# A cross network on one core: bias sums moved and put into another bank, third input block moved, and one row matmul in place of two

## The chip, the cores and the metric

The kernel runs on one core of one Trainium2 chip. The core has five engines that matter here: PE (TensorE, matmuls and their weight loads), DVE (VectorE), ACT (ScalarE), POOL (GpSimd) and SP (SyncE, which here only issues transfers). The metric is the device time of the launch in microseconds (us); a lower time is better. Six runs of the kernel before gave a median of 130.84 us (130.69 to 130.98).

## The reference

The reference is a stack of six cross layers. With `x0` of shape 4096 x 416, weights `ws` of shape 6 x 416 x 416 and biases `bs` of shape 6 x 416, all in bfloat16:

```python
x = x0
for l in range(6):
    x = x0 * (x @ ws[l] + bs[l]) + x
```

Both kernels carry the sum differently. After layer l, the result is x0 times (everything that the layers so far contributed, plus the running sum of the biases). So the kernel leaves the contraction sums of all layers in the accumulators (PSUM) and adds only each layer's new product to them. It needs the running sums of the bias rows, one column per layer, as a per-feature scalar: that is `cb_sb`, and making it is what the text calls the bias sums.

## The kernel before

**Tiling.** Features are on partitions, batch rows on columns. The 4096 rows are cut into NS = 4 blocks of 1024, each in two halves of 512. The 416 features are three chunks of 128 plus a tail of 32. The tail of a block lies in four lanes of 32 partitions, one per quarter (256 rows) of the block. In each lane the first 256 columns hold the lane's own quarter and the second 256 hold its neighbour's quarter (lane g holds the quarter of lane g^1).

**A layer on PE** has these stages, in this order (n = 6s + l counts the 24 layers):

- Half A: nine contraction steps, each of four matmuls side by side in column tiles (128 x 32), 512 columns (`step`, recorded at L201).
- The row phase (L343): the tail's 32 features contracted into the chunks. It runs in four row tiles (32 x 128), one lane each. Part 0 covers chunk 0 (even lanes) and chunk 2 (odd lanes), part 1 covers chunk 1 (even lanes) and the tail's own output (odd lanes). An even lane does one matmul of 512 columns per part. An odd lane does two of 256 columns per part, because the neighbour's quarter sits in the second half of its buffer. So a row phase has 12 matmuls. The last one raises `s_ti`, on which DVE's half A of the layer waits.
- Tail outputs (12 matmuls of 256 columns, L201), which raise `s_to`.
- Half B: nine more steps.

DVE then turns each of the six accumulators into the next `x` with one operation of 128 x 512 (L444): add the bias scalar, multiply by x0. ACT (L496), POOL (L188) and ACT again (L478, `swap_lanes`) do the same for the tail and copy it to the neighbour lanes. The next row phase waits for DVE's six (`s_xb`) and for the swap (`s_sw`).

**The start.** Block 0 is loaded row by row and turned on PE, since its turned form is wanted at once. `xin_sb` holds six groups of 128 rows in three transfers (h = 0, 1 and the "third input block", groups 4 and 5); groups 6 and 7 come turned by a transposing transfer. PE runs 14 filler matmuls (L210), then 12 turns of 128 x 128 (L239) in the order `IN_ORDER`, into six banks, of which DVE copies chunks 0 and 2 (`s_inD`) and ACT chunk 1 (`s_inA`). Then, in PE's order:

1. the bias sums: 16 small matmuls of `bsa_sb` with a triangle of ones `u_sb`, into bank 1 (L248 to L254). They raise `s_cbp`; ACT copies bank 1 to `cb_sb` (L465) and raises `s_cb`;
2. contraction step 0 of half A (k = 0), chunk by chunk. Chunk m = 1 accumulates in bank 1, so it waits for `s_cb` (before m = 1);
3. `third_input()`: 24 matmuls into banks 6, 7 and 3, copied by DVE (L424) and ACT (L475);
4. step k = 1; `tail_inputs()` (16 matmuls, raising `s_tp`; copied by ACT at L482 and DVE at L426, `s_te` and `s_te0`); step k = 2;
5. the row phase of layer 0, behind waits for all copies (`s_inD` 6, `s_inA` 3, `s_te`, `s_te0`, `s_cb`) and for the tail's weights (`s_wt`, `s_wtp`).

The order on each engine is written out by hand. PE works through its program in order, and a wait holds all that is behind it; the same holds for ACT, DVE and POOL. The transfers go out on three queues: SP's, ACT's and POOL's. The tail weights of layer 0 come in four pieces by `load_wt`: lanes 1 and 3 from ACT, lanes 0 and 2 from POOL, where they stand ahead of the four `wc_sb` transfers (L173).

The functions that the diff touches, with the line numbers of the profile:

Of the kernel before, what the change touches and what calls it, by code (L numbers as in the profile page):

```python
# [8 lines left out]
ACTF = mybir.ActivationFunctionType  # L9


def bass_standalone__dcn_v2_cross__recsys_kernel(
# [20 lines left out]
    with ExitStack() as es:  # L33
# [58 lines left out]


        IN_BANKS = ((3, 4, 6), (0, 5, 7))
        IN_ORDER = ((0, 0), (0, 1), (1, 0), (1, 1), (0, 2), (1, 2))
        THIRD = (6, 7, 3)
        HALVES = (slice(0, 64), slice(64, 128))

# [12 lines left out]
        @block.sync  # L111
        def _(sp):
            sp.dma_start(xin_sb[:, 0:2, :], x0_v[:, 0:2, :]).then_inc(s_xin[0], 16)
            sp.dma_start(w_sb[:, 0, 0, :], ws[0, 0:128, :]).then_inc(s_w0, 16)
            sp.dma_start(xin_sb[:, 4:6, :], x0_v[:, 4:6, :]).then_inc(s_xin[2], 16)
            sp.dma_start_transpose(x0T_sb[:, :, 768:SB], x0[768:SB, 0:DF]).then_inc(s_x0T[0], 16)
            for l in range(1, L):
                sp.dma_start(w_sb[:, l, :, :], wmain(l)).then_inc(s_w[l], 16)
                if l == 1:
                    for g in range(4):  # L120
                        load_wt(sp, g, 1, L, s_wt[1])
            for s in range(1, NS):
                sp.dma_start_transpose(
                    x0T_sb[:, :, s * SB:(s + 1) * SB], x0[s * SB:(s + 1) * SB, 0:DF]
                ).then_inc(s_x0T[s], 16)
                sp.dma_start_transpose(
                    x4_sb[:, s - 1:s, :], x0[s * SB:(s + 1) * SB, D - 128:D]
                ).then_inc(s_x4[s - 1], 16)
            for s in range(NS - 1):
                n = (s + 1) * L  # L130
                sp.wait_ge(s_xa, NC * n)
                sp.wait_ge(s_xb, NC * n)
                for c in range(NC):
                    sp.dma_start_transpose(
                        o_sb[:, s * JS:(s + 1) * JS, c * 128:(c + 1) * 128], xo_sb[:, s, c, :]
                    ).then_inc(s_oT, 16)
                sp.wait_ge(s_xt, n)
                sp.dma_start_transpose(ot_sb[:, s, :, :], xot_sb[:, s, :]).then_inc(s_ot, 16)
                sp.wait_ge(s_oT, 16 * NC * (s + 1))
                sp.wait_ge(s_otc, s + 1)  # L140
                sp.dma_start(
                    out_v[:, s * JS:(s + 1) * JS, :], o_sb[:, s * JS:(s + 1) * JS, :]
                ).then_inc(s_out, 16)
            j = (NS - 1) * JS
            sp.wait_ge(s_oeA, 2)
            sp.dma_start(out_v[:, j:j + 4, 0:256], o_sb[:, j:j + 4, 0:256]).then_inc(s_out, 16)
            sp.wait_ge(s_oeA, 3)
            sp.wait_ge(s_oet, 1)
            sp.dma_start(out_v[:, j:j + 4, 256:D], o_sb[:, j:j + 4, 256:D]).then_inc(s_out, 16)
            sp.wait_ge(s_oeD, 1)  # L150
            sp.wait_ge(s_oeA, 4)
            sp.dma_start(out_v[:, j + 4:j + 6, :], o_sb[:, j + 4:j + 6, :]).then_inc(s_out, 16)
            sp.wait_ge(s_out, 16 * (NS + 3))

        @block.gpsimd
        def _(pool):
# [8 lines left out]
                out=u_sb[:, :], in_=ones_sb[0:L + 1, 0:L], pattern=[[1, L]],  # L165
                compare_op=ALU.is_ge, fill=0.0, base=1, channel_multiplier=-1,
            ).then_inc(s_set, 1)
            for g in (0, 2):
                load_wt(pool, g, 0, 1, s_wtp)
            pool.wait_ge(s_zero, 1)  # L170
            for i, (a, b) in enumerate(((0, 1), (1, L))):
                for g in (1, 3):
# [26 lines left out]
        def _(pe):  # L199
# [33 lines left out]
            fill(14)  # L233
            pe.wait_ge(s_set, 1)
            for i, (h, c) in enumerate(IN_ORDER):
                if i in (0, 2):
                    pe.wait_ge(s_xin[h], 16)
                for j in range(2 * h, 2 * h + 2):
                    ins = pe.transpose(  # L239
                        out=psT[:, IN_BANKS[h][c], (j % 2) * 128:(j % 2 + 1) * 128],  # L240
                        in_=xin_sb[:, j, c * 128:(c + 1) * 128], identity=ident[:, :],
                    )
                ins.then_inc(s_inT, 1)

            pe.wait_ge(s_bs, 16)
            pe.wait_ge(s_zero, 2)
            pe.wait_ge(s_set, 2)
            for c in range(NC):  # L248
                for q in range(4):
                    f0 = c * 128 + 32 * q  # L250
                    tile_mm(ps[32 * q:32 * q + 32, 1, c * 8:c * 8 + L], bsa_sb[:, f0:f0 + 32], u_sb[:, :], q, True)
            for q in range(4):
                ins = tile_mm(ps[32 * q:32 * q + 32, 1, NC * 8:NC * 8 + L], bsa_sb[:, DF:D], u_sb[:, :], q, True)
            ins.then_inc(s_cbp, 1)  # L254

            def out_chunk(c):
                for j in range(4):
# [7 lines left out]
            for s in range(NS):  # L265
                for l in range(L):
# [34 lines left out]
                    if n == 0:  # L301
                        pe.wait_ge(s_w0, 16)
                        for k in range(NC):
                            if k == 1:
                                pe.wait_ge(s_w[0], 16)
                                third_input()
                            if k == 2:
                                pe.wait_ge(s_xtl0, 16)
                                tail_inputs()
                            before_a(k)  # L310
                            for m in range(NC):
                                if k == 0 and m == 1:
                                    pe.wait_ge(s_cb, 1)
                                step(m, 0, k)
                    else:
                        if s == 0:
                            pe.wait_ge(s_w[l], 16)
                        chunk(0, 0, before_a)
                        chunk(1, 0)
                        chunk(2, 0)  # L320

                    if n == 0:
                        pe.wait_ge(s_inD, 6)
                        pe.wait_ge(s_inA, 3)
                        pe.wait_ge(s_te, 1)
                        pe.wait_ge(s_te0, 1)
                        pe.wait_ge(s_cb, 1)
                    else:
                        pe.wait_ge(s_xb, NC * n)
                        if l == 0:  # L330
                            pe.wait_ge(s_xt, n)
                            pe.wait_ge(s_te, s + 1)
                        else:
                            pe.wait_ge(s_sw, s * (L - 1) + l)
                    if s == 0 and l < 2:
                        if l == 1:
                            pe.wait_ge(s_wc[1], 32)
                        pe.wait_ge(s_wt[l], (32, 64)[l])
                    if n == 0:
                        pe.wait_ge(s_wtp, 32)  # L340

                    def row(g, dst, lhsT, cols, start):
                        return pe.matmul(  # L343
# [4 lines left out]
                    lo, hi = slice(0, G), slice(G, 2 * G)  # L348
                    for part in range(2):
                        if n == 0 and part == 1:  # L350
                            pe.wait_ge(s_wc[0], 32)
                        for h in range(2):
                            g, wm = 2 * h, slice(part * 128, part * 128 + 128)
                            row(g, ps[:, NC * h + part, :], wt_sb[lane(g), l, wm], slice(0, H), h == 1)
                            g += 1
                            if part == 0:
                                row(g, ps[:, NC * h + 2, hi], wt_sb[lane(g), l, 0:128], lo, h == 1)
                            else:
                                row(g, ps[:, 6 + h, lo], wc_sb[lane(g), l, 0:128], lo, True)
                        for h in range(2):  # L360
                            g = 2 * h + 1
                            if part == 0:
                                ins = row(g, ps[:, NC * h + 2, lo], wt_sb[lane(g), l, 0:128], hi, False)
                            else:
                                ins = row(g, ps[:, 6 + h, lo], wc_sb[lane(g), l, 32:160], hi, False)
                    ins.then_inc(s_ti, 1)
                    if n == 0:
# [90 lines left out]
        def _(act):  # L458
# [2 lines left out]
            act.dma_start(xtl_sb[:, :, :], x0_v[:, 6:JS, DF:D]).then_inc(s_xtl0, 16)  # L461
            for g in (1, 3):
                load_wt(act, g, 0, 1, s_wt[0])
            act.wait_ge(s_cbp, 1)
            act.activation(  # L465
                out=cb_sb[:, :, :],
                in_=ps[:, 1, 0:8 * (NC + 1)].rearrange("p (c e) -> p c e", e=8)[:, :, 0:L], func=ACTF.Copy,
            ).then_inc(s_cb, 1)
            for h in range(2):
                act.wait_ge(s_inT, 2 * h + 2)  # L470
                act.activation(
                    out=x0T_sb[:, 1, h * 256:(h + 1) * 256], in_=psT[:, IN_BANKS[h][1], 0:256], func=ACTF.Copy
                ).then_inc(s_inA, 1)
# [6 lines left out]

            act.wait_ge(s_tp, 1)
            act.activation(out=x0t_sb[:, 0, 0:G], in_=ps[:, 5, 0:G], func=ACTF.Copy).then_inc(s_te, 1)  # L482
            act.wait_ge(s_cb, 1)
            for s in range(NS):
                for l in range(L):
# [75 lines left out]
```

## Time and profile before

| What | Value |
|---|---|
| Median of six runs | 130.84 us (130.69 to 130.98) |
| Time of the profiled execution | 130.98 us |
| Its span, first to last instruction | 129.2 us |
| PE busy | 124.5 us (96% of the span) |
| DVE, ACT, POOL busy | 100.5, 71.3, 23.3 us |
| Mean granted clock of PE | 0.996 |
| Last filler matmul ends, row phase of layer 0 begins | 4.00 us, 8.56 us |
| One layer from then on (row phase to row phase) | 4.88 us, layer 0 to 1: 4.95 us |
| Row phases in the chain | 0.55 us each; layer 0: 0.62, layer 1: 0.66 |

The profiled execution's time is 1.78 us above its span (130.98 less 129.2): what lies outside the first and last instruction. Times inside the profile are counted from the span's start. A group of matmuls in four tiles appears as overlapping records; the distance from one group's start to the next is what it costs, not the duration of one record (0.379 us for 512 columns).

### The profile page before, as it was taken

The numbers are of one execution on the slowest core, as the hardware profiler recorded it, in microseconds if no ns is written. First come the engines' busy times: TensorE is split into PE (matmuls) and PEld (weight loads), VectorE is DVE, ScalarE is ACT, GpSimd is POOL, SyncE is SP. The second block draws the span as 40 slices with busy tenths as digits, with TensorE's granted clock in tenths as the row PEclk, the third lists the DMA queues.
The fourth block names the chain that finished last, engine by engine and source line by source line (L and its number), as shares of the span: only waits on it lengthen the run. The fifth ranks groups of instructions, "written<-read, shape, count | busy, mean of one in ns | idle before, by whom it ended". The sixth has DMA issues, their size and how long they took to land.

```text
span 129.2 us, 5416 instructions
## 1 busy us (share of the span) xinstructions
PE 124.5 (96%) x2454; PEld 64.7 (50%) x2454; DVE 100.5 (78%) x154; ACT 71.3 (55%) x164; POOL 23.3 (18%) x42
## 2 busy tenths in 40 slices
PE   7999999999999999999999999999999999999980
PEld 5654454554545545545545545545545545545550
DVE  2349779779779779779779779779779789789790
ACT  0627356376736456476745555475745555555680
POOL 7802102102102022012012022012022032022130
PEclk9999999999999999999999999999999999999998
DMA  3999899996009808000008534000009907000026
GB/s 99 310 283 306 202 119 223 112 235 62 5 5 106 168 0 269 0 0 5 0 5 164 105 109 160 5 0 0 5 0 89 185 0 264 5 0 5 3 82 186
DMA packets 32918, 12.54 MB, mean 97 GB/s; under 512 B 25338, under 2 KB 32896, under 8 KB 32896
## 3 DMA queue, kind: packets, MB, share of 16 engines
q1 hardware_dynamic: 31488, 11.47, 43.5%
q10 hardware_dynamic: 1184, 0.67, 1.7%
q8 instruction: 19, 0.31, 1.0%
q0 software_dynamic: 224, 0.06, 0.2%
q14 instruction: 3, 0.02, 0.1%
HBM read 2.90 MB, written 3.41 MB: 49 GB/s over the span
## 4 chain that ended last, share of the span: by engine, by line
PE 96%; DVE 1%; issue 0%; DVEq 0%
PE ps L201 82%; PE ps L343 10%; PE ps L210 2%; PE ps L239 1%; DVE o_sb L449 1%; PE ps L393 0%; DVEq L33 0%
## 5 line engine op out<-in xcount | busy, mean ns | idle before, releaser
L444 DVE SCALAR_TENSOR_TENSOR xT_sb<-ps,cb_sb,x0T_sb 128x512 bf16<-128x512 f32 x120 | 80.9, 743 | 16.9 <-PE ps L343 16.9
L201 PE MATMUL ps<-xT_sb,w_sb 128*32 128x512 bf16 (+1 forms) x1680 | 89.0, 364 | 0.0
L201 PEld LDWEIGHTS ps<-xT_sb,w_sb 128*32 128x32 bf16 x1680 | 43.1, 97 | 38.6 <-issue 4.2
L478 ACT ACTIVATE xt_sb<-xt_sb 32x256 bf16<-32x256 bf16 x80 | 33.1, 414 | 16.6 <-POOL xt_sb L188 15.9
L496 ACT ACTIVATE t_sb<-ps,cb_sb 64x256 f32<-64x256 f32 x48 | 22.5, 468 | 30.7 <-PE ps L201 30.4
L188 POOL TENSOR_TENSOR xt_sb<-t_sb,x0t_sb 128x256 bf16<-128x256 f32 x20 | 13.4, 671 | 80.4 <-ACT t_sb L496 80.4
L201 PE MATMUL ps<-x0T_sb,w_sb 128*32 128x512 bf16 (+1 forms) x336 | 18.8, 365 | 0.0
L444 DVE SCALAR_TENSOR_TENSOR xo_sb<-ps,cb_sb,x0T_sb 128x512 bf16<-128x512 f32 x23 | 15.6, 743 | 3.4 <-PE ps L343 3.3
L343 PE MATMUL ps<-xt_sb,wt_sb 32*128 32x512 bf16 (+1 forms) x160 | 12.2, 327 | 0.0
L201 PEld LDWEIGHTS ps<-x0T_sb,w_sb 128*32 128x32 bf16 x336 | 8.4, 97 | 7.4 <-issue 0.8
L509 ACT ACTIVATE x0t_sb<-x_sb 32x256 bf16<-32x256 bf16 x24 | 9.9, 413 | 0.4
L343 PE MATMUL ps<-xt_sb,wc_sb 32*128 32x256 bf16 x80 | 7.7, 268 | 0.0
L343 PEld LDWEIGHTS ps<-xt_sb,wt_sb 32*128 32x128 bf16 x160 | 2.5, 92 | 8.6 <-DVE xT_sb L444 8.5
L188 POOL TENSOR_TENSOR xot_sb<-t_sb,x0t_sb 128x256 bf16<-128x256 f32 x4 | 2.7, 672 | 12.6 <-ACT t_sb L496 12.6
L343 PEld LDWEIGHTS ps<-xt_sb,wc_sb 32*128 32x128 bf16 x80 | 4.0, 93 | 0.4
L210 PE MATMUL ps<-const-bfloat16-1.0 128*128 128x256 bf16 x14 | 3.1, 418 | 0.8 <-PEq L546 0.8
L419 DVE COPY x0T_sb<-ps 128x256 bf16<-128x256 bf16 x4 | 1.1, 292 | 2.8 <-PE ps L239 2.5
L465 ACT ACT_TABLE_LOAD x1 | 1.3, 1283 | 3.5 <-issue 3.5
L210 PEld LDWEIGHTS ps<-const-bfloat16-1.0 128*128 128x128 bf16 x14 | 2.0, 145 | 1.6 <-issue 0.8
L343 PE MATMUL ps<-x0t_sb,wt_sb 32*128 32x512 bf16 (+1 forms) x32 | 2.4, 326 | 0.2 <-issue 0.2
L173 POOL DMA_DIRECT2D wc_sb<-in_ws_dram x4 | 2.2, 548 | 0.0
L517 ACT ACTIVATE o_sb<-ps 128x512 bf16<-128x512 f32 x3 | 1.8, 597 | 0.3 <-PE ps L201 0.3
(41 smaller groups left out, 24.0 us busy)
## 6 DMA issues: line engine op xcount, KB each, us to landing
out_dram<-o_sb SPq DMA_DIRECT2D x3, 832.0 KB, 4.1
w_sb<-in_ws_dram SPq DMA_DIRECT2D x5, 312.0 KB, 5.7
xin_sb<-in_x_dram SPq DMA_DIRECT2D x2, 208.0 KB, 3.5
out_dram<-o_sb SPq DMA_DIRECT2D x1, 256.0 KB, 2.3
xin_sb<-in_x_dram ACTq DMA_DIRECT2D x1, 208.0 KB, 3.3
w_sb<-in_ws_dram ACTq DMA_DIRECT2D x1, 208.0 KB, 3.6
out_dram<-o_sb SPq DMA_DIRECT2D x1, 208.0 KB, 2.3
out_dram<-o_sb ACTq DMA_DIRECT2D x1, 208.0 KB, 2.7
```

Of the source, the lines that this page charges most:

```text
L173: pool.dma_start(wc_sb[lane(g), a:b, 32 * g:32 * g + 32], ws[a:b, DF:D, DF:D].rearrange("l p n -> p l n")).then_inc(s_wc[i], 16)
L188: pool.tensor_tensor(out=dst, in0=t32_sb[:, n % 2, :], in1=x0t_sb[:, s, 0:G], op=ALU.mult).then_inc(s_xt, 1)
L201: return pe.matmul(dst, lhsT=lhsT, rhs=rhs, start=start, stop=True, skip_group_check=True, tile_position=(0, 32 * q),)
L210: pe.matmul(ps[:, 7, 0:256], lhsT=const[:, 0:128], rhs=const, start=True, stop=True)
L239: ins = pe.transpose(out=psT[:, IN_BANKS[h][c], (j % 2) * 128:(j % 2 + 1) * 128], in_=xin_sb[:, j, c * 128:(c + 1) * 128], identity=ident[ ...
L343: return pe.matmul(dst, lhsT=lhsT, rhs=srct[lane(g), cols], start=l == 0 and start, stop=True, skip_group_check=True, tile_position=(32 * ...
L444: dve.scalar_tensor_tensor(out=dst, in0=ps[:, NC * half + c, :], scalar=cb_sb[:, c, l:l + 1], in1=x0T_sb[:, c, o:o + H], op0=ALU.add, op1= ...
L465: act.activation(out=cb_sb[:, :, :], in_=ps[:, 1, 0:8 * (NC + 1)].rearrange("p (c e) -> p c e", e=8)[:, :, 0:L], func=ACTF.Copy,).then_inc ...
L478: ins = act.activation(out=buf[lane(g), G:2 * G], in_=buf[lane(g ^ 1), 0:G], func=ACTF.Copy)
L496: ins = act.activation(out=t32_sb[HALVES[h], n % 2, :], in_=tail(h), func=ACTF.Identity, bias=cb_sb[HALVES[h], NC, l:l + 1],)
L509: ins = act.activation(out=x0t_sb[lane(g), s + 1, swap * G:(swap + 1) * G], in_=x4_sb[96:128, s, r * G:(r + 1) * G], func=ACTF.Copy,)
L517: act.activation(out=o_sb[:, j0:j0 + 4, c * 128:c * 128 + 128], in_=ps[:, c, :].rearrange("p (j d) -> p j d", d=128), func=ACTF.Copy,).the ...
```

## The change

- **Bias sums.** They become a function `bias_sums()`, called after `tail_inputs()`, before step k = 2. They write bank 6 in place of bank 1. Bank 6 holds the third input block's chunk 0 at that time, so they wait for DVE's fifth copy (`s_inD` 5). ACT's copy to `cb_sb` moves behind its tail copy. Chunk m = 1 of step k = 0 no longer waits for `s_cb`; that wait now stands before part 1 of the row phase of layer 0, which overwrites bank 6.
- **Third input block.** `third_input()` moves from before step k = 1 to before step k = 2.
- **Order of the turns.** `IN_ORDER` takes chunk 0 of both halves first, then chunk 1, then chunk 2. The waits for the transfers and of ACT follow.
- **Odd lanes' chunk 2.** In part 0 an odd lane does one matmul of 512 columns, which reads its buffer's two halves in swapped order, in place of two of 256. A row phase then has 10 matmuls, in all 24 layers.
- **One transfer.** The tail weights of lane 0 go from POOL's queue to SP's, behind the third input block and ahead of the transposing transfer.

```diff
-        IN_ORDER = ((0, 0), (0, 1), (1, 0), (1, 1), (0, 2), (1, 2))
+        IN_ORDER = ((0, 0), (1, 0), (0, 1), (1, 1), (0, 2), (1, 2))
...
             sp.dma_start(xin_sb[:, 4:6, :], x0_v[:, 4:6, :]).then_inc(s_xin[2], 16)
+            load_wt(sp, 0, 0, 1, s_wt[0])
...
-            for g in (0, 2):
-                load_wt(pool, g, 0, 1, s_wtp)
+            load_wt(pool, 2, 0, 1, s_wtp)
...
-                if i in (0, 2):
+                if i in (0, 1):
                     pe.wait_ge(s_xin[h], 16)
...
-            pe.wait_ge(s_bs, 16)
-            pe.wait_ge(s_zero, 2)
-            pe.wait_ge(s_set, 2)
-            for c in range(NC):
-                for q in range(4):
-                    f0 = c * 128 + 32 * q
-                    tile_mm(ps[32 * q:32 * q + 32, 1, c * 8:c * 8 + L], bsa_sb[:, f0:f0 + 32], u_sb[:, :], q, True)
-            for q in range(4):
-                ins = tile_mm(ps[32 * q:32 * q + 32, 1, NC * 8:NC * 8 + L], bsa_sb[:, DF:D], u_sb[:, :], q, True)
-            ins.then_inc(s_cbp, 1)
+            def bias_sums():
+                pe.wait_ge(s_bs, 16)
+                pe.wait_ge(s_zero, 2)
+                pe.wait_ge(s_set, 2)
+                pe.wait_ge(s_inD, 5)
+                for c in range(NC + 1):
+                    for q in range(4):
+                        f0 = c * 128 + 32 * q if c < NC else DF
+                        ins = tile_mm(ps[lane(q), 6, c * 8:c * 8 + L], bsa_sb[:, f0:f0 + 32], u_sb[:, :], q, True)
+                ins.then_inc(s_cbp, 1)
...
                             if k == 1:
                                 pe.wait_ge(s_w[0], 16)
+                            if k == 2:
                                 third_input()
-                            if k == 2:
                                 pe.wait_ge(s_xtl0, 16)
                                 tail_inputs()
+                                bias_sums()
                             before_a(k)
                             for m in range(NC):
-                                if k == 0 and m == 1:
-                                    pe.wait_ge(s_cb, 1)
                                 step(m, 0, k)
...
                         pe.wait_ge(s_te0, 1)
-                        pe.wait_ge(s_cb, 1)
...
-                        pe.wait_ge(s_wt[l], (32, 64)[l])
+                        pe.wait_ge(s_wt[l], (48, 64)[l])
                     if n == 0:
-                        pe.wait_ge(s_wtp, 32)
+                        pe.wait_ge(s_wtp, 16)
...
                         if n == 0 and part == 1:
+                            pe.wait_ge(s_cb, 1)
                             pe.wait_ge(s_wc[0], 32)
...
                             if part == 0:
-                                row(g, ps[:, NC * h + 2, hi], wt_sb[lane(g), l, 0:128], lo, h == 1)
+                                pe.matmul(
+                                    ps[:, NC * h + 2, :], lhsT=wt_sb[lane(g), l, 0:128],
+                                    rhs=srct[lane(g), :].rearrange("p (b r) -> p b r", b=2)[:, ::-1, :],
+                                    start=l == 0 and h == 1, stop=True, skip_group_check=True, tile_position=(32 * g, 0),
+                                )
                             else:
                                 row(g, ps[:, 6 + h, lo], wc_sb[lane(g), l, 0:128], lo, True)
                         for h in range(2):
                             g = 2 * h + 1
-                            if part == 0:
-                                ins = row(g, ps[:, NC * h + 2, lo], wt_sb[lane(g), l, 0:128], hi, False)
-                            else:
+                            if part == 1:
                                 ins = row(g, ps[:, 6 + h, lo], wc_sb[lane(g), l, 32:160], hi, False)
...
-            act.wait_ge(s_cbp, 1)
-            act.activation(
-                out=cb_sb[:, :, :],
-                in_=ps[:, 1, 0:8 * (NC + 1)].rearrange("p (c e) -> p c e", e=8)[:, :, 0:L], func=ACTF.Copy,
-            ).then_inc(s_cb, 1)
             for h in range(2):
-                act.wait_ge(s_inT, 2 * h + 2)
+                act.wait_ge(s_inT, h + 3)
...
             act.activation(out=x0t_sb[:, 0, 0:G], in_=ps[:, 5, 0:G], func=ACTF.Copy).then_inc(s_te, 1)
+            act.wait_ge(s_cbp, 1)
+            act.activation(
+                out=cb_sb[:, :, :],
+                in_=ps[:, 6, 0:8 * (NC + 1)].rearrange("p (c e) -> p c e", e=8)[:, :, 0:L], func=ACTF.Copy,
+            ).then_inc(s_cb, 1)
```

## The prediction

> **What bounds the kernel now.** I read the chain that ended last first, then the waits, then two row phases and the start in the timeline. The chain (start us, us, what):
>
> ```profile
> 5.41 2.98 PE ps L201 x91
> 8.39 0.17 issue
> 8.56 0.62 PE ps L343 x8
> 9.18 4.33 PE ps L201 x77
> 13.51 0.66 PE ps L343 x8
> 14.17 4.33 PE ps L201 x84
> 18.49 0.55 PE ps L343 x8
> 19.04 4.33 PE ps L201 x84
> ```
>
> From 8.56 us on nothing but PE stands in it: 0.55 + 4.33 = 4.88 us a layer, to 124.57 us. So a row phase that is shorter by d gives 24 d, if DVE keeps up. The waits:
>
> ```profile
> DVE xT_sb L444 <- PE ps L343: 16.9, 20, 1.1
> PEld ps L343 <- DVE xT_sb L444: 8.5, 20, 0.4
> PEld ps L201 <- issue: 5.0, 24, 0.2
> ```
>
> The second line looks as if DVE held PE before each row phase. It doesn't: in the trace's records the first row weight load comes 0.307 us after the last column-tile matmul began in nearly every layer, while DVE's end lies 0.143 to 0.172 us ahead of it, and in layer 1 only 0.071. The constant is PE's own[...]. DVE has at least 0.07 us a layer to spare.
>
> Weight loads of the row phases of layers 1 and 2:
>
> ```profile
> 13.43 0.33 PEld L343 LDWEIGHTS ps<-xt_sb,wt_sb 32*128 32x128 bf16 x7 [0.42 <-DVE xT_sb L444]
> 13.67 0.09 PEld L343 LDWEIGHTS ps<-xt_sb,wc_sb 32*128 32x128 bf16 x1
> ...
> 18.42 0.12 PEld L343 LDWEIGHTS ps<-xt_sb,wt_sb 32*128 32x128 bf16 x8 [0.42 <-DVE xT_sb L444]
> ```
>
> In layer 2 eight loads are through in 0.12 us; in layer 1 there is a hole. By the records the tenth instruction, lane 1's second matmul, comes 0.231 us after the first load instead of 0.127. That is why this phase takes 0.66 us and not 0.55. The start:
>
> ```profile
> 5.34 0.17 PEld L201 LDWEIGHTS ps<-u_sb,bsa_sb 7*32 7x32 bf16 x16 [0.20 <-DMA bsa_sb<-in_bs_dram]
> 5.53 0.10 PEld L201 LDWEIGHTS ps<-x0T_sb,w_sb 128*32 128x32 bf16 x4
> 5.92 0.12 PEld L201 LDWEIGHTS ps<-x0T_sb,w_sb 128*32 128x32 bf16 x8 [0.29 <-ACT cb_sb L465]
> 6.15 0.55 PEld L201 LDWEIGHTS ps<-ident,xin_sb 128*32 128x32 bf16 x24
> ```
>
> The bias sums cost 5.53 - 5.34 = 0.19 us of PE, and the wait for ACT's copy 0.18 more: chunk 1 starts 0.39 us after chunk 0, where two groups are otherwise 0.215 apart.
>
> [...] the swapped read keeps two runs of 256 neighbours[...]. No read of this shape stands in the trace.
>
> **The change part by part**, against the profiled execution (span 129.2 us, time 130.98; the median is 130.84).
>
> *Row phases.* An odd lane's part 0 goes from two matmuls to one of the same columns: 2.5 ns less. In the records part 0 holds the even lanes for 0.226 us (4 ns after the first load to 230) and the odd ones for 0.229 (7 to 236), so the even lanes cap what is left: part 1's odd matmuls move up by about 3 ns, and with them the phase's end. 24 x 2.5 ns = 0.06 us. From below, the seam costs x ns in each lane. The nearest thing seen is the first matmul after an emptied array, 11 ns over the others (0.120 against 0.109 us for 256 columns). 24 x (11 - 2.5) = 0.20 us slower. From above, no more than 3 ns x 24 = 0.07. I take 0.06 faster.
>
> *Layer 1's hole.* After the change the first nine instructions are four loads, four matmuls and one load, and the tenth is part 1's first matmul. It isn't due before 0.230 us after the first load, and the hole ended at 0.231. What delays this phase, the swap's late semaphore (13.26 us) after which PE's instructions come in two bursts, stays. I take 0.10 us gained; 0 if the hole sits elsewhere.
>
> *Turns.* The second pair now needs the other half, whose transfer landed at 4.10 us (records). PE was to load its weights at 4.03 and now waits to about 4.14; after the gap the next matmul follows faster (0.064 instead of 0.107 us, as at 3.97), so the last turn stays at 5.10 within 0.03. DVE's second copy comes at 4.98 instead of 5.11, ACT's two by about 5.5, since its table load ends at 4.74. Neither is late.
>
> *Start.* Step k = 0 begins where the bias sums did, 5.34. [...] Steps 0 and 1 are six groups: 6 x 0.2155 + 0.02 = 1.31, to 6.65. The third input takes 6.70 - 6.36 = 0.34, the tail inputs 7.57 - 7.34 = 0.22: to 7.21. Now the new wait. Bank 6 is free when DVE has copied the third input's chunk 0. Before, that copy began 0.34 after the third input and signalled 0.435 later, so now at 6.65 + 0.775 = 7.43. A wait of PE's own took 0.10 us from the semaphore to the weight load (transfer landed 3.83, load at 3.94): 7.53. PE stands for some 0.3 us. Bias sums 0.19: 7.72. Step 2's last group starts 0.44 later, the drain is 0.31: row phase at 8.48 to 8.52, against 8.56. So 0.37 us removed, 0.3 put back by the new wait: 0.05 gained. Queued behind that wait are step 2 and everything after it; the work that might hide it, the tail inputs, already runs ahead of it.
>
> *The other waits.* DVE's tail copy is third in its row at 0.34 each after 6.99, done at 8.11. PE needs 0.276 after that (8.254 to 8.530 before), so 8.39, ahead of 8.48. `cb_sb`: last bias matmul 7.62, 0.22 to its semaphore, ACT 0.2: 8.1, long before part 1 of the row phase. Were this cover gone, each would cost what it is late, once.
>
> *Transfers.* SP's extra issue (about 0.45 us) moves all that is behind it on SP: the transposing transfer lands at 8.1 instead of 7.61, wanted at 9.05; layer 1's weights at 8.55 instead of 8.09, wanted near 11.2; its tail weights at 10.5, wanted at 13.4. Lane 0's piece, issued at 2.3 like ACT's (landed 6.45 and 7.11), is there before 8.4. POOL's come 0.55 earlier. Cost nothing; gone cover would show as a PE wait at these places.
>
> *Sum.* 0.05 + 0.10 + 0.06 = 0.21 us: span 129.0, median 130.84 - 0.21 = 130.63 us.
>
> **Rivals.**
> *Second burst in the bias sums.* If layer 1's hole is what PE does after any long wait, the bias sums get it too: first eight instructions, then up to 0.2 us nothing. For: PE will have waited there 0.3 us or more with its queue empty. Against: 22 other row phases follow such a wait without a visible hole. Then -0.21 + 0.20: 130.83; if layer 1's hole stays as well, 130.93.
> *The seam costs (slower).* Place: the swapped read in each odd lane's part 0. Everything behind it in the phase moves, 24 times, with no cover, since PE sets each layer. From 0.26 us slower than before on, it needs (0.26 + 0.15 + 2.5 x 0.024)/24 = 20 ns, about the time of 48 columns. At 30 ns: 24 x 0.030 = 0.72, less 0.15: 131.4. For: the shape is untried in this trace. Against: both runs are contiguous[...].
> *More than I count.* The fillers run at half rate (3.15 us for 14 x 256 columns, 0.21 each); full rate comes at about 5.37 by the records. Where it comes earlier, the turns shorten, the old kernel still waits for its bias rows (landed 5.17) and ACT, and the new one doesn't: 0.1 to 0.2 more, 130.45. Where it comes later, the new start, all contraction, suffers more: up to 0.1 back.
>
> **How the numbers follow.** About 0.2%, 0.26 us, is what a measurement of this kernel can tell from no change. As forecast (130.50 to 130.75): 0.55, of which 0.2 below 130.58, since the forecast lies near that limit. More gained: 0.13. Second burst or hole kept (130.75 to 131.0): 0.17. Seam: 0.15, nearly all slower. So faster 0.33, same 0.52, slower 0.15. Range 130.40 to 131.05: it takes in the bursts and the 11 ns seam (130.63 + 0.06 + 0.20 = 130.89), and leaves out the dear seam and the last of the gain. The forecast's own range is 130.50 to 130.75.
>
> **What would show it.** Right: step k = 0 at 5.34 with no wait for `cb_sb`; PE idle about 0.3 us before the bias sums, released by DVE's L424; row phase of layer 0 at 8.5; layer 1's row phase near 0.55; all others 2 or 3 ns shorter, period still 4.87; DVE's idle before L444 unchanged. Wrong: a row phase longer than 0.55 (seam), a hole among the bias sums' loads, a start of step 0 well off 5.34, or the row phase of layer 0 held by L426 or by a landing.

## The result, and the profile after

The changed kernel takes 131.72 us (median of 33 runs, 130.70 to 132.54). The kernel before took 130.92 us beside it (70 runs, 130.68 to 132.04). The ratio is 1.0062, with a 95% interval of 1.0050 to 1.0074: slower by 0.6%. Medians here are over all executions; ratios leave out those more than 1.5% above the fastest of their kernel, and aren't quotients of the medians. The forecast, 130.63 us with a range of 130.40 to 131.05, was wrong.

The profiled execution of the changed kernel took 131.03 us, so it is a quick one of its kind. Its span is 129.2 us, the same as before, and yet it is put together differently. The chain that ended last (start us, us, what), first and last pieces:

```profile
4.87 2.13 PE ps L201 x64
7.08 1.02 PE ps L201 x28
8.10 0.32 PE ps L341
8.64 4.33 PE ps L201 x84
12.97 0.32 PE ps L341
13.52 4.33 PE ps L201 x84
...
123.86 0.57 PE ps L394 x8
124.45 0.69 DVE o_sb L450
```

The new line numbers: L341 is the row helper, L356 the new 512-column matmul, L394 the last turns of the output, L450 a copy of it. PE enters its last turns at 123.86 us, where the kernel before did so at 124.57. By the records PE's last matmul comes at 124.56 us instead of 125.27: PE is done 0.71 us earlier. The span ends at the same time. So 0.69 us were lost after PE's last matmul. From there to the end of the span, which is called the closing stretch below, it takes 4.65 us, before 3.96.

Weight loads of the start in the changed kernel (start us, us, what, and in brackets the idle time ahead and what ended it):

```profile
4.84 0.37 PEld L201 LDWEIGHTS ps<-x0T_sb,w_sb 128*32 128x32 bf16 x12 [0.19 <-issue]
...
7.05 0.20 PEld L201 LDWEIGHTS ps<-u_sb,bsa_sb 7*32 7x32 bf16 x16 [0.22 <-issue]
7.27 0.34 PEld L201 LDWEIGHTS ps<-x0T_sb,w_sb 128*32 128x32 bf16 x12
8.03 0.09 PEld L341 LDWEIGHTS ps<-x0t_sb,wt_sb 32*128 32x128 bf16 x1 [0.42 <-issue]
```

Step k = 0 begins at 4.87, without a wait for `cb_sb`. The bias sums stand behind a gap of 0.22 us. The row phase of layer 0 begins at 8.03 instead of 8.56. Layers 1 and 2, the same columns:

```profile
12.90 0.09 PEld L341 LDWEIGHTS ps<-xt_sb,wt_sb 32*128 32x128 bf16 x1 [0.43 <-DVE xT_sb L445]
12.90 0.09 PEld L356 LDWEIGHTS ps<-xt_sb,wt_sb 32*128 32x128 bf16 x1
...
12.95 0.28 PEld L341 LDWEIGHTS ps<-xt_sb,wc_sb 32*128 32x128 bf16 x3
17.77 0.09 PEld L341 LDWEIGHTS ps<-xt_sb,wt_sb 32*128 32x128 bf16 x1 [0.42 <-DVE xT_sb L445]
```

Layer 1 is no longer longer than the others: from row phase to row phase it takes 4.87 us by the difference of these two lines. In the records the median period is 4.872 us instead of 4.875. The waits (who waited for whom: us in all, times, longest):

```profile
DVE xT_sb L445 <- PE ps L341: 16.9, 20, 1.2
PEld ps L341 <- DVE xT_sb L445: 8.5, 20, 0.4
```

They are those of before, so no new wait of PE or DVE recurs in the layers. What differs is the end. Four transfers carry the last output: SP's of 256, 160 and 208 KB, in this order, and one of ACT. The profile's list of transfers (KB of one, us from issue to landing) has this line for the first, of 256 KB, in the changed kernel:

```profile
out_dram<-o_sb SPq DMA_DIRECT2D x1, 256.0 KB, 3.4
```

and this one in the kernel before:

```profile
out_dram<-o_sb SPq DMA_DIRECT2D x1, 256.0 KB, 2.3
```

The end of the timeline shows the issues of the 256 KB (L146, after the change L147) and of the 160 KB (L149, then L150). First the kernel before:

```profile
124.26 0.37 SPq L146 DMA_DIRECT2D out_dram<-o_sb  x1
...
125.16 0.69 DVE L449 COPY o_sb<-ps 128x1024 bf16<-128x1024 bf16 x1
...
125.45 0.37 SPq L149 DMA_DIRECT2D out_dram<-o_sb  x1
```

then the changed kernel:

```profile
123.55 0.37 SPq L147 DMA_DIRECT2D out_dram<-o_sb  x1
...
124.45 0.69 DVE L450 COPY o_sb<-ps 128x1024 bf16<-128x1024 bf16 x1
...
124.74 0.72 SPq L150 DMA_DIRECT2D out_dram<-o_sb  x1
```

Both issues begin 0.71 us earlier than before, but the second takes 0.72 us instead of 0.37, and the 256 KB land later (126.91 instead of 126.61 us by the records). The records have 16 landings for a transfer and the profile counts 16 DMA engines, so I read them as one part for each engine. Before, parts 15 and 16 of the 256 KB landed at 126.57 and 126.61. After, they landed at 125.88 and 126.91: one part of 16 is a full microsecond behind.

The records name what else moves then. Instructions come by DMA too, in this line of the queues in both kernels (packets, MB, share of 16 engines):

```profile
q8 instruction: 19, 0.31, 1.0%
```

By the records each of the 19 packets has 16 KB. The queue isn't named after an engine. I read the packets as fetches of PE's program: PE has 4812 recorded loads and matmuls in the changed kernel, 253 for each packet, and every other engine fewer than 300 instructions in all. And from the start of one packet to the start of the next, PE goes on by 249 records on average (252 in the kernel before). So I take a packet to bring one block of PE's instructions, some 250 of them by this estimate, and call the place where a block begins its edge. In the changed kernel the last such packet runs from 123.98 to 125.05 us, and the 256 KB transfer's own packets start at 124.46: they overlap by 0.59 us. In the kernel before it ran from 123.28 to 124.62 us, and the first packet of the 256 KB started 0.55 us later, at 125.17. The change takes 48 matmuls and 48 weight loads from PE's program, and the last packet comes later relative to PE's end: it starts 0.6 us ahead of the last matmul instead of 2.0.

### The profile page after: what moved, and what is told of

It reads as the page before. It is cut to its first block, busy times and chain, and to the rows that moved or that the text cites. A ratio compares the mean times of both kernels' runs of the same rounds, so it can differ in the third digit from the quotient of the medians.

```text
span 129.2 us, 5323 instructions
## 1 busy us (share of the span) xinstructions
PE 123.8 (96%) x2406; PEld 62.0 (48%) x2406; DVE 100.3 (78%) x154; ACT 71.4 (55%) x164; POOL 22.7 (18%) x41
## 4 chain that ended last, share of the span: by engine, by line
PE 96%; DVE 1%; DVEq 0%; issue 0%
PE ps L201 82%; PE ps L341 10%; PE ps L210 2%; PE ps L239 1%; DVE o_sb L450 1%; PE ps L394 0%; DVEq L33 0%; PE ps L356 0%
## 5 line engine op out<-in xcount | busy, mean ns | idle before, releaser
L341 PE MATMUL ps<-xt_sb,wt_sb 32*128 32x512 bf16 x80 | 12.2, 380 | 0.0
L356 PE MATMUL ps<-xt_sb,wt_sb 32*128 32x512 bf16 x40 | 7.8, 385 | 0.0
L341 PE MATMUL ps<-xt_sb,wc_sb 32*128 32x256 bf16 x80 | 7.7, 268 | 0.0
L341 PEld LDWEIGHTS ps<-xt_sb,wt_sb 32*128 32x128 bf16 x80 | 2.3, 92 | 8.5 <-DVE xT_sb L445 8.5
L341 PEld LDWEIGHTS ps<-xt_sb,wc_sb 32*128 32x128 bf16 x80 | 4.0, 93 | 2.3
L341 PE MATMUL ps<-x0t_sb,wt_sb 32*128 32x512 bf16 x16 | 2.4, 380 | 0.0
```

Source lines behind the costliest of these rows:

```text
L341: return pe.matmul(dst, lhsT=lhsT, rhs=srct[lane(g), cols], start=l == 0 and start, stop=True, skip_group_check=True, tile_position=(32 * ...
L356: pe.matmul(ps[:, NC * h + 2, :], lhsT=wt_sb[lane(g), l, 0:128], rhs=srct[lane(g), :].rearrange("p (b r) -> p b r", b=2)[:, ::-1, :], star ...
```

## The experiments

Four theories stand in the expectations. **F** (fetch at the end): fewer PE instructions push PE's last fetch (one such 16 KB packet) beside the output transfers. **G** (edge in the start): in the changed start a block edge of PE's program falls behind the wait for bank 6, so an early fetch is asked for late and PE runs dry in layer 1. **S** (start): the new start, all contraction, suffers more from a late full clock. **Q** (queue): lane 0's weights on SP's queue delay what is behind them. All kernels compute the whole result. Ratios are to the kernel before, run beside them.

**One matmul undone, and one matmul alone.** The first keeps the new start and goes back to two matmuls:

```diff
-                                pe.matmul(
-                                    ps[:, NC * h + 2, :], lhsT=wt_sb[lane(g), l, 0:128],
-                                    rhs=srct[lane(g), :].rearrange("p (b r) -> p b r", b=2)[:, ::-1, :],
...
+                                row(g, ps[:, NC * h + 2, hi], wt_sb[lane(g), l, 0:128], lo, h == 1)
...
-                            if part == 1:
+                            if part == 0:
+                                ins = row(g, ps[:, NC * h + 2, lo], wt_sb[lane(g), l, 0:128], hi, False)
+                            else:
```

> The changed kernel with the odd lanes' chunk 2 as two matmuls of 256 columns again (96 PE instructions more); the new start stays. Theory F (PE's 16 KB instruction fetches fall at other times once its stream is 96 instructions shorter, and the last one meets the last output transfers on one DMA engine): back at the time of the kernel before or a little under it, 130.6 to 130.9 us. Theory S (the new start costs, since it is all contraction and so suffers where full clock comes late): still slow, 131.4 to 131.8. Theory Q (the extra transfer on SP's queue moves what follows on it or changes which DMA engines the last transfers use): still slow, 131.4 to 131.8.

The second is the kernel before with only the new matmul:

```diff
-                                row(g, ps[:, NC * h + 2, hi], wt_sb[lane(g), l, 0:128], lo, h == 1)
+                                pe.matmul(
+                                    ps[:, NC * h + 2, :], lhsT=wt_sb[lane(g), l, 0:128],
+                                    rhs=srct[lane(g), :].rearrange("p (b r) -> p b r", b=2)[:, ::-1, :],
...
-                            if part == 0:
-                                ins = row(g, ps[:, NC * h + 2, lo], wt_sb[lane(g), l, 0:128], hi, False)
-                            else:
+                            if part == 1:
```

> The kernel before with the one 512-column matmul alone (96 PE instructions fewer); the old start and the old queues. Theory F: slow, 131.4 to 131.9 us, with the last transfer landing about 4.5 us or more after PE's last matmul. Theories S and Q: as the kernel before less 24 x 3 ns, 130.8.

Measured: two matmuls 131.09 us, ratio 1.0008 (0.9989 to 1.0027), above the 130.6 to 130.9 that F expected; one matmul alone 131.49 us, 1.0034 (1.0020 to 1.0047), beside 130.94. So the row edit that saves PE time makes the kernel before slower. The profile of one matmul alone has the layers as forecast: period 4.872 us, no hole in layer 1, last matmul at 125.12, 0.15 us earlier than in the kernel before. And its span is 0.36 us longer. The end of its timeline, with the issue of the 160 KB, and its line of the 256 KB transfer:

```profile
125.31 0.61 SPq L149 DMA_DIRECT2D out_dram<-o_sb  x1
```

```profile
out_dram<-o_sb SPq DMA_DIRECT2D x1, 256.0 KB, 3.2
```

The slow issue (0.61 us) and the slow landing are back. The last fetch runs from 124.54 to 125.49, 0.47 us into the packets of the 256 KB; their parts 15 and 16 land at 126.45 and 127.30. With two matmuls and the new start they land together (126.29 and 126.32), and the closing stretch is 3.96 us. In the closing stretch F stands; S and Q say nothing of it. The median with two matmuls isn't clear of the changed kernel's in the same series (131.20 us, below), so that F's saving shows in its profile and not in its median.

**The changed kernel again, and lane 0 back on POOL's queue.** The changed kernel was run beside these two without an edit:

> The changed kernel unaltered, for a second profile beside the others on the same chip. All theories: 131.7 us, between 130.7 and 132.5 from one execution to the next. F expects that the profile shows the last output transfers' landing late, one DMA engine behind the others. S expects PE's last matmul itself to come late.

Lane 0's weights back:

```diff
-            load_wt(sp, 0, 0, 1, s_wt[0])
...
-            load_wt(pool, 2, 0, 1, s_wtp)
+            for g in (0, 2):
+                load_wt(pool, g, 0, 1, s_wtp)
...
```

> The changed kernel with lane 0's tail weights back on POOL's queue. Theory Q: back at 130.6 to 130.9 us. Theories F and S: still slow, 131.4 to 131.8.

Measured: again 131.20 us, 1.0016 (0.9995 to 1.0036, 14 runs). Lane 0 back 132.18 us, 1.0093 (1.0059 to 1.0126, 6 runs), slower than any theory expected. Q falls: without its extra transfer the kernel is slower. Note that the same kernel gave 1.0062 in one series and 1.0016 in another, outside each other's intervals. The next paragraphs show what varies from one execution to the next; whether the chip plays a part isn't known. Layer 1's row phase in the repeated kernel:

```profile
13.09 0.09 PEld L341 LDWEIGHTS ps<-xt_sb,wt_sb 32*128 32x128 bf16 x1
13.66 0.09 PEld L341 LDWEIGHTS ps<-xt_sb,wc_sb 32*128 32x128 bf16 x1 [0.48 <-issue]
```

and with lane 0 back on POOL:

```profile
13.39 0.09 PEld L341 LDWEIGHTS ps<-xt_sb,wt_sb 32*128 32x128 bf16 x1
14.42 0.09 PEld L341 LDWEIGHTS ps<-xt_sb,wc_sb 32*128 32x128 bf16 x1 [0.93 <-issue]
```

PE stops for 0.36 and 0.81 us, counted from matmul to matmul, always between the same two instructions, "for issue": no semaphore is late. The records show the first fetch of the stream from 11.26 to 12.17 us in the one and from 11.78 to 12.92 in the other. PE goes on 1.49 and 1.50 us after its end, by the weight load. In the changed kernel's first profile that fetch ended at 11.45. 1.49 later is 12.94, just when the instruction was due (12.95), and there is no hole. This is G's picture of PE running dry. Both closing stretches are long too (4.53 and 4.39 us), as F says.

The place can be counted. In PE's records (loads, matmuls and waits) the late instruction is the 450th in both. In two other profiles PE stands at record 706, in layer 2 (0.12 us lost with two matmuls, 0.06 with the last kernel below), which is 256 records on. So I estimate one edge every 256 records: 450, 706, 962 and so on. In the ten profiles of this document none of 180 such edges is passed less than 1.39 us after the end of its packet. Six are passed 1.39 to 1.50 us after it, four at record 450 in layer 1 and the two at 706. At five of these PE stands, and in the changed kernel's first profile it comes just in time. By the same count the last packet would bring records from 5058 on, where the changed kernel's end at 4859: by this estimate what collides at the end is a fetch ahead that no recorded instruction uses.

**Moving the edges without touching the work.** If F and G are right, idle PE instructions must make the kernel faster. The first kernel puts waits that are long satisfied into half B of 18 layers (72 more wait instructions on PE by the records), which moves the late edges only:

```diff
                     for m in range(NC):
+                        if n >= 6 and m == 0:
+                            for done, v in ((s_set, 2), (s_zero, 2), (s_ones, 1), (s_cbp, 1), (s_tp, 1), (s_te0, 1), (s_cb, 1), (s_inA, 3), (s_inD, 6)):
+                                pe.wait_ge(done, v)
```

> The changed kernel, the same matmuls, with nine waits more in PE's program ahead of half B in layers 6 to 23, all satisfied long before: some 70 instructions that cost PE's array nothing. Theory F (PE's last 16 KB instruction fetch meets the last output transfers): the fetch starts 1 us or more earlier against PE's last matmul, the last transfer lands about 3.6 us after that matmul instead of 4.2, and the median falls by 0.4 to 0.6 us against the changed kernel's run in this call or 131.2 to 131.7. The start stays, so executions still spread by over 1 us. Rival (the late landing comes from the read shape or the shorter row phase, not from the stream's length): unchanged, 131.2 to 131.7.

The second makes the fill of 28 matmuls of 128 columns instead of 14 of 256, the same columns but 28 more PE instructions ahead of every edge:

```diff
-                    pe.matmul(ps[:, 7, 0:256], lhsT=const[:, 0:128], rhs=const, start=True, stop=True)
+                    pe.matmul(ps[:, 7, 0:128], lhsT=const[:, 0:128], rhs=const[:, 0:128], start=True, stop=True)
...
-            fill(14)
+            fill(28)
```

> The changed kernel with the filler as 28 matmuls of 128 columns in place of 14 of 256: the same time, 28 instructions more at the front, so that the edge of PE's instruction block that fell on the bias sums (behind their wait) is crossed among the third input or tail inputs, before the wait. Theory G (the fetch of the next block is asked for too late there and layer 1 runs out of instructions): no hole in the row phase of layer 1, first fetch seen near 9 us instead of 10.2 to 11.8, executions spread less; median 0.2 to 0.5 us under the changed kernel. The end is half mended. Rival (the holes come from late data or semaphores): hole stays.

The third has both edits:

> Both of the two edits above. F and G together: 130.3 to 130.6 us, under the kernel before, with a spread like that kernel's. If only one is right: 130.8 to 131.2. If neither: 131.2 to 131.7.

The fourth has both, and moves the bias sums, with their wait, two groups later:

```diff
                                 tail_inputs()
-                                bias_sums()
                             before_a(k)
                             for m in range(NC):
                                 step(m, 0, k)
+                                if k == 2 and m == 1:
+                                    bias_sums()
```

> Both edits, and the bias sums placed after chunk 1 of step k = 2, by when the wait for bank 6 is over. The wait of 0.25 to 0.4 us ahead of the bias sums goes: 0.2 to 0.3 us under the kernel with both edits, 130.0 to 130.4 us; if the row phase of layer 0 is then held by the tail copies or by the bias copy, 0.1 of that is lost.

Measured, beside 131.04 us of the kernel before (67 runs):

| kernel | median us (runs) | ratio, 95% | profiled: closing stretch, hole in layer 1, first fetch starts |
|---|---|---|---|
| idle waits late | 130.84 (22) | 0.9983 (0.9964 to 1.0003) | 3.97, 0.96, 12.12 |
| fine fill | 131.23 (14) | 1.0005 (0.9980 to 1.0030) | 3.96, none, 7.98 |
| both | 130.74 (22) | 0.9978 (0.9961 to 0.9994) | 3.96, none, 7.55 |
| both, bias sums later | 130.91 (22) | 0.9972 (0.9954 to 0.9989) | 3.96, none, 8.95 |

The changed kernel wasn't run beside these, and they ran on another chip than the four above. Neither of the last two reached its forecast, and the later bias sums bring no gain that the medians show. All four have the short closing stretch again. In the fine fill's end SP has the same code as in the changed kernel, and the same times up to the issue of the 160 KB:

```profile
124.74 0.37 SPq L150 DMA_DIRECT2D out_dram<-o_sb  x1
```

```profile
out_dram<-o_sb SPq DMA_DIRECT2D x1, 256.0 KB, 2.5
```

Its last fetch ran from 123.28 to 124.27 us and was over 0.18 us before the first packet of the 256 KB. PE's last matmul is at 124.56 in this kernel and in the changed one, layers and row phases are alike, and the span is 128.5 against 129.2 us. That is the price of the collision by itself: 0.69 us for the place of one 16 KB packet. Over the profiles the loss follows the overlap. In the changed kernel, its repetition, one matmul alone and lane 0 back, fetch and 256 KB packets overlap by 0.59, 0.52, 0.47 and 0.35 us, and the closing stretch is longer than before by 0.69, 0.57, 0.51 and 0.43. In the other six the fetch was over 0.18 to 0.67 us before, and the stretch is 3.96 to 3.97 us.

The idle waits leave the early edges alone. The profiled execution is the slowest of its 22 (131.86 us), and it has the hole of layer 1, the largest:

```profile
13.54 0.09 PEld L341 LDWEIGHTS ps<-xt_sb,wt_sb 32*128 32x128 bf16 x1
14.71 0.09 PEld L341 LDWEIGHTS ps<-xt_sb,wc_sb 32*128 32x128 bf16 x1 [1.08 <-issue]
```

The fetch ended at 13.24; PE went on 1.47 us later. With the fine fill the fetch starts at 7.55 to 8.95 us, and no hole in layer 1 is left. The two last kernels beat the kernel before, by 0.2 to 0.3%.

Why the first fetch comes late is less clear. That a fetch is asked for one block ahead of its edge is the author's estimate. One block ahead of the 450th record, at the 194th, PE is in the bias sums in the changed kernel, at 7.08 us. The kernel before reaches its 194th no sooner (7.14), and its fetch starts at 9.54. The kernel with two matmuls has the changed kernel's start, wait included, and its fetch starts at 9.12; in the others with that start and the coarse fill it is 10.25 to 12.12. A rival is that the fetch queues behind other transfers, which keep the DMA engines busy until then and longer (in the kernel before, a share of 0.97 from 20 to 32 us, and 0.33 from 32 to 60). In the ten profiles the first four fetches start 2.4 us (median) after PE is one block ahead of their edge, the later ones 0.5 us. So that a late packet starves PE is shown; that the wait for bank 6 makes it late is supported by the fine fill, not shown.

A second new wait shows in the start of the profile with idle waits:

```profile
6.72 0.34 PEld L201 LDWEIGHTS ps<-ident,xin_sb 128*32 128x32 bf16 x24 [0.83 <-DMA xin_sb<-in_x_dram]
```

The third input block's transfer isn't there when step k = 1 is done; PE stood 0.71 us at 6.01 in the records (0.57 in the kernel with the bias sums later). The row phase of layer 0 then began at 8.65 us, later than before the change.

**What stays open.** How many of the 0.8 us of the median are the hole and how many the clock can't be said, since only single executions have a profile. What delays the early fetch was tested by moving the edge ahead of the wait for bank 6, not by taking the wait away or the other transfers. The row edit with idle waits alone, in the old start, wasn't measured, nor the later bias sums alone. Why the fine fill alone has the higher median, with the same closing stretch as the others, is open; the intervals overlap.

## Why the prediction was wrong

The profiles add up, so each step can be set against its own size (us against the kernel before's profile; below nothing is faster):

| term | forecast | first profile | repeated | lane 0 on POOL |
|---|---|---|---|---|
| row phase of layer 0 begins | -0.05 | -0.53 | -0.35 | -0.11 |
| layer 1's hole, net of the 0.11 before | -0.10 | -0.11 | +0.25 | +0.70 |
| 23 later row phases | -0.06 | -0.07 | -0.07 | -0.07 |
| after PE's last matmul | 0 | +0.69 | +0.57 | +0.43 |
| span | -0.21 | -0.02 | +0.40 | +1.02 |

(The last column adds to 0.95. Of the rest, 0.06 is the row phase of layer 0, where part 1 waited for `wc_sb`: behind lane 0's piece on POOL's queue it landed at 8.59 us, in the changed kernel at 7.63.) The median, 131.72, is 0.80 above the kernel before's beside it. That lies between the second and the third of these executions.

- **Row phases: right in the array, wrong in the sum.** The forecast was 2.5 ns a phase, as much as the records of the kernel before give between two groups of 256 columns (0.2183 us from start to start) and one of 512 (0.2158); the period fell by 3 ns, and DVE's waits are unchanged. So the rival "The seam costs (slower)" is out: the swapped read costs nothing that can be seen. But the step counted the two matmuls removed only as array time. It left out that 96 instructions fewer move PE's fetches.
- **"Transfers … Cost nothing": this is the step that failed.** It went through the kernel's own transfers, queue by queue, and left out the one queue that isn't in the code, the instructions' own. The page before showed it ("q8 instruction"). Both ends of it cost: the last fetch, 0.4 to 0.7 us in each of the four profiles with the row edit and unmoved edges, and the first one, 0 to 0.8 in those of them that have the new start. No rival named either. The chance given to slower, 0.15, was for the seam; that slower came true isn't to that rival's credit.
- **Start: right at its own clock.** From step k = 0 to the row phase of layer 0 the forecast worked out 3.16 us (5.34 to 8.50) and the profile has 3.16 (4.87 to 8.03), with the gap of 0.2 to 0.3 us before the bias sums and DVE's copy shortly ahead of it. What moved is the start of step 0, one of the forecast's own signs of being wrong; that it would be where the bias sums had begun was the author's estimate. The full clock came at 3.98 us in this execution and at 5.37 in the one before, and the turns took 0.83 us in the chain instead of 1.41. So the earlier step 0, by 0.47 us, is in good part the luck of this execution. How much of it the old start would have had, which waits for its bias rows (landed at 5.17), wasn't profiled. With the full clock at 5.07 (lane 0 on POOL) the row phase gains 0.11, at 4.67 it gains 0.35: this is the rival "More than I count", right in its direction. With idle waits it didn't hold: full clock at 4.14, and the row phase 0.09 later, behind the third input block.
- **Layer 1's hole: right in size in the first profile, wrong in its reason.** The 0.10 us went, as worked out. The forecast put it down to two bursts after the swap's semaphore. But the instruction that came late in the kernel before is the 450th of PE's records too, at the block's edge, where the holes of 0.36 to 0.96 us in the other profiles ended 1.5 us after the fetch. With one matmul alone in the old start, the weight load at the 451st record still comes 0.20 us later than in other layers, but nothing waits for it, as the forecast's count says. With the fine fill, where the edge lies elsewhere, no load of this phase is late. Why the instruction was late before isn't shown: its fetch had ended at 10.57, 3.09 us ahead.
- **"Second burst in the bias sums"** as named is out: the 16 loads there are through in 0.20 us.
- **Waits for `cb_sb`, DVE's tail copy and lane 0's weights** cost nothing, as worked out.

## What to carry to other kernels

An edit that removes instructions from a long unrolled program can also move the fetches of its instructions: here 96 fewer put the start of the last one 0.6 us ahead of PE's last matmul instead of 2.0. Look in the trace for the last fetch of each busy engine and ask what shares the DMA engines with it then; and for the first ones ask how long before its edge each packet ends, and whether a wait or other transfers hold it up. If an edit makes the bound engine finish earlier and the span doesn't follow, compare the landing of the last transfer, part by part: here 15 of 16 parts were on time. Where a fetch is in the way, a few idle instructions ahead are a way to move it: the 72 here brought the closing stretch back to 3.97 us.

## What the runs showed of the hardware

- One fetch of 16 KB takes about 1 us (0.88 to 1.34 us for the last fetch of ten profiles). Where it overlapped the packets of the 256 KB output, one part of 16 landed 0.79 to 1.03 us after the others, and SP's issue of the next transfer took 0.51 to 0.72 us instead of 0.37. That the late part and the fetch are on the same DMA engine is inferred: the records don't name the engine.
- Where PE was short of instructions, it went on 1.39 to 1.50 us after the end of the packet (five holes in ten profiles); at no edge did it go on sooner.
- The full clock came at 3.7 to 5.4 us in ten profiles of kernels with the same or nearly the same start, and lasted 122.88 us where it ended inside the span; after that the records grant 0.5. From these two figures and the span and mean clock of each execution, the start of the full clock, called the release here, can be estimated: span, less 2(1 - clock) of the span, less 122.88. It fits nine of the ten profiles within 0.15 us; in the tenth, the one with idle waits, the clock stayed full to the end and the estimate fails. By it the median of the changed kernel's executions rises from 131.0 us (release at 3 to 4 us, three executions) to 132.2 (6 to 7), that of the kernel before from 130.8 (4 to 5) to 131.1 (6 to 7). But the two ran in different series. In the last series alone, without the executions at clock 1.0, a straight line through the estimates gives 0.30 us for each us of later release in the kernel before, 0.30 to 0.34 in the three kernels with the fine fill, which have the new start too, and 0.41 with idle waits alone. So S isn't shown; what is steeper goes with the kernels that can have the hole.
